# Attention and a cosine feed-forward in one kernel: scores of three units at a time, masks as products, tables ahead of loads

## The chip, the cores and the metric

The kernel runs on one core of a Trainium2 chip. The metric is the device time of one execution in microseconds. The engines that matter here: PE multiplies matrices into PSUM (eight banks), ACT (ScalarE) evaluates exponentials and sines and copies, DVE (VectorE) does elementwise work, POOL (GpSimd) makes small tables and issues the casting loads, and SP issues stores and transposing transfers.

## What is computed

Sliding-window attention with a linear distance bias for 8 batches, 8 heads, 576 positions and 64 features a head, and then a feed-forward layer with h * cos(h) as its activation:

```python
scores = scale * np.matmul(q, k.transpose(0, 1, 3, 2))          # scale = 1/8
rel = pos[:, None] - pos[None, :]
bias = slopes[:, None, None] * (-np.abs(rel))[None, :, :]       # slopes[h] = 2 ** -(h + 1)
mask = (rel >= 0) & (rel < 128)
scores = np.where(mask, scores + bias[None], -1e9)
attn = softmax(scores); x = attn @ v                            # x: 4608 tokens by 512
h = x @ w_in                                                    # 512 by 2048
out = (h * np.cos(h)) @ w_out                                   # 2048 by 512
```

## The kernel before

**Units.** Attention is cut into units of one batch, one pair of heads and one group of 256 query positions (G = 0 or 1), and a tail unit ("t") that holds the last 64 positions of all four pairs; nine units a batch. For each unit `scores` (L485 to L516) multiplies keys by queries. A head has 64 features, so the two heads of a pair lie in the two row halves of PE, each half writing a bank of its own: a unit of G = 0 is 2 x 256 + 2 x 128 columns in four matmuls, a unit of G = 1 has six matmuls, a tail sixteen. This mode of PE, with 64 active rows, is entered and left for every call of `scores`. `exps` (L521) takes the exponential on ACT into a buffer `p`, `mask` (L543) multiplies by `emask` on DVE, which holds exp(slope * distance) inside the window and 0 outside, `pv` (L567) multiplies by V with a column of ones that gives the sums, `norm` or `norm_two` divides on DVE (L632, L634 for one unit, L647, L649 for two at once), and `x_pe`, `x_pe_two` or `x_dma` transposes the result into `xT`.

**Chunks.** The 4608 tokens go through the feed-forward in nine chunks of 512. `moe1` (L738 PE, L744 ACT, L748 DVE), or `moe1_half` (L762, L767, L771) for chunk 0, makes g = h cos(h) bank by bank. `moe2` multiplies by `w_out`: plainly for chunk 0 (L823), else with seven products of sums of blocks (L879), whose sums `gsum` DVE makes (L813). Attention of later batches runs beside it: after the hidden layer of chunk c come QUOTA[c] units (9, 9, 11, 10, 10, 9, 5), an "exp phase", since ACT has to load another table between sines and exponentials. The first nine units run before chunk 0. Scores use banks 4 to 7 (`SB`), P times V banks 2 and 3 (`UB`), the output products banks 0 and 1 (`OB`); the hidden layer uses `UB` and `SB`.

**Order.** Nothing is ordered by hand. Each operation is recorded with the keys it reads and writes; `schedule` then reads a start time for each from the packed table `STARTS`, and with it, for operations that either ACT or DVE may do, the engine. On each engine the instructions stand in the order of these times, and waits are put where a dependence crosses engines.

**Head.** SP loads the first 256 positions of q in float32 (`load_first_q`, L317), which ACT and DVE cast (L321, L322). POOL issues, in this order: the first piece of k (L310), the identity (L374, L375), the second pieces of q and k (L310), the table of distances `dif` (`distances`, L381 to L388; float32, -1e6 outside the window), V and the four pieces of w_in (L329, L361), later loads. ACT makes the eight `emask` tables from `dif` (L431). PE runs nine warm-up products (L416), transposes q and k (L451), runs two more warm-ups, and starts on the scores; after the first two units come four `KEEP` products (L424), whose results nobody reads.

Of the kernel before, what the change touches and what calls it, by code (L numbers as in the profile page):

```python
# [30 lines left out]
    "c-o~_3v?7k7M%_O>$I}lyrVd&jB%(mF^)}$p`BmNBm)V<BtVRC3?U#pXoN{bfe~0_v#^HGLJXi7CH^2HBJ28J`M7FSR7Auzi"  # L31
    ">`PMD)?FS99B_8k|mkxecj0<nM?@iHl(NORn@C{_uY4^O@bCR#hzFzDnu_Z4LqqOM~tp!(zK43spEgAsq-12zXU-OPMJDJyG"
    "FE5pIUcU(+yf&S3rvpGe%5F#&6Q;gj4l!eBQRcM$dPi)^96f>ViXy3f+TUK??Ex_?UZoi}ePy7=cHHq$I;%TQatPH1&QW2^O"
    "tae}Jjg)c4bK!)TW`!4wg?M|;lc-=g*2U5i1e^=S8%0HKFT5F)~9wCJ7oq;rJU(~YU$Ap5fjNoV4^-LPssAdUm*EFfy}tAw*"
    "d7Qeoe16pEPbn`{)>S^6W#(6tWlXONuxu9u6i;kjBnHaLa0G)FilG}P);_)*m7dcDZ9r(4!VE#V{ro|J?*tM+_n`EuW83*8="
    "$!EHk4mzc89Ua&%w4zMuwl?8htQz#+Ux8CER0I<_)th;J>Pw`Lb42=R3H`3^f7EoIqwzE~c!-XZP4ReKaJtJ=QY6~LYnxudT"
    "2iY{OZ;n3P_N#|Cq;gFg(m<lm=Y-(O(<wBR?0%mA|%X7w3yCfF~!QV>om#H_IMI@6sj?)>zYk!F?DkAoO~M8`pY?ZK}&+x#p"
    "eL?Gq5G$8t8fpv5GY%jK*Icf~h~Pi>cRu_HIiL6+I)IF9yFxuY^QixA&I&<kLd$ghu1FUq~cRzZN0h4<e8h!7$s-eSb&KX-E"
    "t)p|FI+vN_$?oiFI0cikzBBz_SjUWbCQs`K<h*V?FHeB)@5gwsZPom=a?pW<gldkI%GAqK4vFwSNxxl}uTDU+G;{NSb*k0(P"
    "ue9_kjYX@!n!8R%o@C5?1%#Evp&F1C<({f&|`0Ww%oY7al^-RnAKA+Fy#@B)XK5wroS^Ag2O-gFoo%RzFNRV%~o4>i{LS<7%"  # L40
    "C7V_^mZgr8TIC_G!+9UbZx(uvjCNqxk#;JzFvt7Sq?-p%gk$PuG}qE#|FL!Rdk5wDUrKIDL_#)9-3V?{PAb5bpD#*i$x=e&U"
    "Z!Q(0+RVer9Mey#ijf`4-pl#nfX_SjewayrcxlF+iv%hDr`}6-lK}TfGHC7Ei1%nB}6PW^Vx(_oJMN-ql}^twxYy)t-gZ~f@"
    "VHIbQXxE)JAy<j){a3%5S;$#FoOA6_dYuYF2YJ=)T`MuHa+JZ?!!sy-gQ2R@j_^&Hv=@Mq-pHsah(p-uc(;@AQ~cu0BrvWr2"
    "wel@2(KV?yeE@<Mvtaj`t?OC89~_pBBd1@+dz%a0ZWWfh8nNq#r@3lLSXwg**^=1IT+W_cvY0&7kaG((t45RjIFAEb|G<$RC"
    "9;ABs@gsSDa^o5zO8MuP+9l8fTL@BY?@tdovPfpL<99mbFoHt%%Px-uuB`CJ?JE#gpd7CBh*Lip8#Ncz$DdQjd{fimDQ<Bx3"
    "i8la~m1}QjAla_lh&!?T$@NaJ{g`d^NICzC!?X6kOdnj7KLW-Me?tunuAb|FadMMdv?jaIfwnbrO1Z-Ua{B&2U_t;w|M>cwl"
    "Qr2(-C5bo-9!XEbz;ZMJe`GALM#&K2Fzs2Yg;jim{c(~%S<~P8BBDG7EcB>5pjuObE37>BBi=2GIS19=&8#BwiGH4*NKoT>R"
    "z1+k@p6bO*yTQ15WQ0P?_p|`hJk=_*by0sg6&%e~y0zANe_BVSX1vW94^-WQ1chm0<d3D*;&8yRrcB$kQZx(G2hJK`mf;&p*"
    "s$tM|TK%2?i7Spuu~x(Ds~RHFIU<o?|@lO0IgZ*x9NS4_G?XUHhue^M*eMMs`lt1~2(wx(^_&=|SxgwBu=sozmc)xNcM%j)|"
    "a)HZzR<?s$k8=ILwOuAvrvA~OgP}-j0(|51VdCr-A>{a5Uo-if&&j5u|(gi3oLL{lKOh14e1FuvP-K+I6nt|_9Std|UC4yxp"  # L50
    "i&!|iv49K{P8wbeNM$N-Yd*YiyAu}?5M_6k?x#%NTM9Z!c7P;jB8rG#{!Q6X8ybB_(e~^bu1RyC+IuBZWfFe^-&s@F<9p0|F"
    "G~<&-a-{Tncij6!;s0pP!QuO*B46)b6tg8m%Yzo)mr)F1N&aHO|Q=z0rS)UR=smq_8(l%!4<bv?|!x62#2X@uVfburqk&Vhb"
    "*TK9cCW=C!5`|ry;j;1i0GUKMe!}wdEDTKVCevrosJb)u<ci?UZRJ%McdxLAn@7iJW8Lgk_(8XBx;on8-x)TSTP9LyWjHkdm"
    "~D`f##aM3{_u>4*0D#Vj`>Pn}|c1gny7ncajd!ACp*+uf1^#Ixk6o)%qU_`OvBC8Cv2F?J$iolBb_PKO1aqdxwwU-CiCPET&"
    "$2oy3&A@-cH!!Re5D8$F75h61@h?U<?j0kLuUr9t8#oeuZIVzMcUW`9ZsG`#$C+{c85KP?dE?kKGz--NA$Ve)xR<04MhmEJ2"
    "+~B;-;+y?%$<t7o`e?(}bzd~jbior9TkJ&_*3kLskS;l>{a>{<=jQS~^pO$pNMp6lxt=~3oIes=6*U%Au2135^`33T&X0oY_"
    "l9XViju{A>~lOdR%WbzQxBQD+PU?_CKBI^q@&mku(6re)I$+0_>;0ZD`wed7sGaG-O~>o=;S#R>*lN|6<^nNiC-n@wEPTpua"
    "?ivT_w%pvtdESK`-|)**@L{Okw=D@&>T+M{vHKJ5))w@*Nb_())obsc!Fwj3UhMNEY-nMGbAekq-;%p0E3M=LgLXIlxu0JEv"
    "%Hc&bC*xG4!qm|0{IMuY519wlG0)#khvuZ4vp&4RNoZOw`)mpj*vug?xOI2)RNBI4HIjGzuX6|pwWbC7Tps7J>Mjbh5Kqd;W"
    "Z6*~pwAQ*M%Hdsi;n3q^+mac_v1P01IkTQOs&ORLoH~wURG~eq4X7g0*k}y>CC^;VA$q-&1R`1VD52;Y1P`B|!bEwwG1uA3k"  # L60
    "H_^;>S>AgV17&<=h^dS}4}Pim-Hr1UydD+;3)%A?fQyiEZ8rT<N%5<y;yv^X!^&S{fOYe?J9jj`^rloHE!*Z%i@e#(9JW^Z`"
    "U;pcMP2Sf;os#+8#6C>cT*dswwjZ=up2>xIom@G6!Zu&2s+%g!MJfdK>(uCMnl?kqlXj$@zVm7C8~&itfon5Ra4r=6p@nZ;`"
    "%b10zpztgDI}lqKW`6E+e^&R?HJsb3qBfM_GJ5qiWqhCo(8y{JSM|>lm*C8q^67%`f+iDdB|=*A%ny_lBzKQT0`}lkxPudVF"
    "o+(wbcFCG3+jJHJA$$NFglH95z7p+u2RZzx;k+*_Ml56*J3MW$zETS=&PiA^jGVk((_e(L{{(V(i!ZYkZA;`$!zjw<-+QZI!"
    "SEN}XW$Y6#{6j4t;^@I5p2ADr87Uwb<^GL5a{<(okkcb|f1frVqeyKhev9S{sFD2A8wMq#+wU5sYQk#9;vKr=Rk5}UD$M`s_"
    "vc&pWUbx7gG4-L^u$1xGPr*_s-gU?iwIA`rMZ4>)-WE{HqWm%%Jjh&YhVCz7eEHW((8?dE`^|3a^&`S&i4_)=LU!qdrsi)*v"
    "Em06a`h8fh*I&QsqS?WT7bk7QGH-f$&jn3txO`Iq8efyVc@b<;y<{BVjsh19d`?PuIdFtenn|PxFhF6`p?4~!4NokPfRh=KO"
    "4TC81rC%Ojy`4_CHg`1$z"
# [153 lines left out]
def bass_alibi_sliding__then__act_gcu_kernel(  # L222
# [8 lines left out]
    with ExitStack() as ctx:  # L231
# [32 lines left out]
        ob = [obuf[:, i, :] for i in range(NOB)]  # L264
        rec = [sb(f"rec{i}", [128, 8], F32) for i in range(2)]
        ident = sb("ident", [128, 128])
        halfpi = sb("halfpi", [128, 1], F32)
        dif = sb("dif", [128, 2, 128], F32)
# [3 lines left out]
        KEEP = 4  # L272
        QUOTA = [9, 9, 11, 10, 10, 9, 5]
# [39 lines left out]
        def load_first_q():  # L313

            t0, R, _ = PIECES[0][0]
            rows = bass.AP(q.tensor, q[0].offset, [[64 * R, 32], [64 * S, H], [1, 64 * R]])
            op("sp", [lambda e: e.dma_start(obuf[:, 0:2, :], rows)],  # L317
               w=[("ob", 0), ("ob", 1)], dma="hwq", occ=60, lat=500)
            for y, eng in enumerate(("dve", "act")):
                o = qB["q"][:, y, 0:512]  # L320
                op(eng, (lambda e, o=o, y=y: e.tensor_copy(o, ob[y])) if y == 0 else  # L321
                   (lambda e, o=o, y=y: e.activation(o, ob[y], ACTF.Copy)),  # L322
                   r=[("ob", y)], w=[("qB", "q", 0, y)], occ=(340, 450)[y], lat=(420, 560)[y],
                   pri=3)

        def load_v(b, order=range(NBLK)):
            for t in order:
# [5 lines left out]
                   occ=900, lat=740 * rows // 100)  # L333
# [94 lines left out]

        def masks():
# [56 lines left out]
        def scores(us, slot):  # L486

            def f(e):
                ins = None
                for n, (b, pr, G) in enumerate(us, slot):  # L490
                    banks = SB[2 * n:2 * n + 2]
                    if pr == "t":
                        for pr in range(NPAIR):
                            for half in range(2):
                                for x in range(2):
# [3 lines left out]
                                                   query_ap(b, x, pr, 4, 64), start=True, stop=True)  # L499
# [4 lines left out]
                    for (c0, c1, kc, qb, nb) in jobs:  # L504
                        for x in range(2):
                            ins = e.matmul(ps[:, banks[x], c0:c1], keys_ap(b, x, pr, kc),  # L506
                                           query_ap(b, x, pr, qb, 128 * nb), start=True, stop=True)
                return ins
            keys, held, occ = [], [], 0
            for n, (b, pr, G) in enumerate(us, slot):  # L510
                keys += tkeys((b, pr, G))
                held += [("B", x) for x in SB[2 * n:2 * n + 2]]
                occ += 250 if pr == "t" else 220 if G else 165
            if us[0] == (0, 0, 0):
                keys.append("warm2")
# [5 lines left out]
        def exps(u, n, table):  # L521
            b, pr, G = u
            banks = SB[2 * n:2 * n + 2]
# [414 lines left out]

        def attention(us, phase):

            for g in range(0, len(us), 2):
                two = us[g:g + 2]
                if phase < 0 or SINGLE:
                    for n, u in enumerate(two):
                        scores([u], n)
                        exps(u, n, 2 * phase + 2)
                        mask(u)
                else:
                    scores(two, 0)
                    for n, u in enumerate(two):  # L950
                        exps(u, n, 2 * phase + 2)
                    for u in two:
                        mask(u)
                if phase < 0 and g == 0:
                    keep()
                sets = [list(zip(two, OB if phase < 0 and g == 0 else UB))]
                if any(u[1] == "t" for u in two):
                    sets = [[s] for s in sets[0]]
                for set_ in sets:
                    pv(set_)  # L960
                    after = []
                    (b, pr, G), _ = set_[0]
                    if (PAIRN and phase >= 0 and len(set_) == 2 and set_[1][0] == (b, pr + 1, G) and set_[0][1] == UB[0]
                            and ucount[0] % 2 == 0):
                        n = ucount[0]
                        ucount[0] += 2
                        norm_two(set_, n)
                        if (S * b + 256 * G) // CH > phase + 1:
                            x_dma(set_[0][0], n)
                            x_dma(set_[1][0], n + 1)  # L970
                        else:
                            x_pe_two(set_, n)
                        continue
# [97 lines left out]
```

The softmax here doesn't subtract the row's maximum and nothing guards it: scores larger than these inputs give would overflow.

## Time and profile before

| | us |
|---|---|
| median of 5 runs | 302.45 (302.04 to 303.46) |
| the profiled execution | 302.49 |
| its span | 300.7 |
| PE busy, 2917 matmuls | 292.2 |
| DVE busy | 245.0 |
| ACT busy | 209.0 |
| POOL busy | 95.1 |
| mean of one L738 matmul of 512 columns | 0.379 |
| mean of one L744 cosine, one L748 product | 0.687, 0.686 |
| mean of an exponential of 128x768, of 128x1024 (L538) | 0.810, 1.025 |
| load of an ACT table | 1.283 |

The page gives for each engine its busy time, and the span in 40 slices of 7.5 us with the busy share in tenths. The timeline lists instructions in order of time, start first and then length, with the number of merged instructions after x and in brackets the idle time before them and what ended it. Matmuls overlap, so the length of a row of matmuls is longer than their spacing; the spacing is read from the starts of successive rows. The windows view gives for a stretch the busy time and count of PE, PE's weight load, DVE, ACT and POOL, then PE's granted clock, the mean share of the 16 DMA engines in use and the GB/s moved.

### The profile page before, as it was taken

What the parts mean: (1) busy time and instruction counts of PE and PEld (TensorE: products, weight loads), DVE (VectorE), ACT (ScalarE), POOL (GpSimd) and SP (SyncE); (2) the same over time, 40 slices, a digit from 0 to 9 for tenths busy, and PEclk for the clock granted to TensorE, in tenths of its full rate; (3) what the DMA queues carried; (4) which work ended last, traced back from release to release, by engine and by line L of the source; (5) the groups of instructions that cost most, each with busy time, mean ns of one, the idle gap of its engine ahead of it and who ended that gap; (6) DMA issues with size and microseconds to landing.
All of it is one profiled execution on the core that took longest, in us unless ns stands there. A gap on an engine that the chain in (4) does not pass through costs nothing.

```text
span 300.7 us, 7145 instructions
## 1 busy us (share of the span) xinstructions
PE 292.2 (97%) x2917; PEld 199.5 (66%) x2917; DVE 245.0 (81%) x513; ACT 209.0 (69%) x302; POOL 95.1 (32%) x122
## 2 busy tenths in 40 slices
PE   7779999999999999999999999999999999999996
PEld 2568745546774588547888886468656865566785
DVE  3878888879977998899988998899879966686781
ACT  5987777488766887787759766778667855755431
POOL 7930992059967501760195014000000000000000
PEclk9999999999999999999999999999999999999999
DMA  7999999999999999999899948972124213102033
GB/s 158 166 200 211 206 167 195 137 165 156 136 188 142 154 173 180 132 174 159 135 147 160 203 40 115 131 175 47 19 46 98 70 20 96 37 0 72 0 124 122
DMA packets 148065, 38.02 MB, mean 126 GB/s; under 512 B 133697, under 2 KB 146753, under 8 KB 148033
## 3 DMA queue, kind: packets, MB, share of 16 engines
q0 software_dynamic: 99344, 18.10, 77.4%
q1 hardware_dynamic: 48688, 19.47, 34.5%
q8 instruction: 23, 0.38, 0.5%
q14 instruction: 10, 0.07, 0.1%
HBM read 36.70 MB, written 9.44 MB: 153 GB/s over the span
## 4 chain that ended last, share of the span: by engine, by line
PE 91%; DMA 6%; POOL 1%; issue 0%; ACT 0%; ACTq 0%; POOLq 0%
PE ps L738 37%; PE ps L879 34%; PE ps L823 5%; PE ps L506 5%; DMA w_inb<-in_moe_w_in_dram 4%; PE ps L762 3%; PE ps L593 2%; DMA krows<-in_k_dram 2%; PE ps L596 2%; PE ps L451 1%; PE ps L497 1%; PE ps L580 1%; PE ps L582 1%; PE ps L700 1%; POOL w_inb L361 0%; PE ps L662 0%
## 5 line engine op out<-in xcount | busy, mean ns | idle before, releaser
L738 PE MATMUL ps<-xT,w_inb 128*128 128x512 bf16 (+1 forms) x576 | 129.0, 355 | 0.0
L744 ACT ACTIVATE cos<-ps,halfpi 128x512 f32<-128x512 f32 x128 | 82.7, 687 | 42.7 <-PE ps L738 30.8
L748 DVE TENSOR_TENSOR gT<-ps,cos 128x512 f16<-128x512 f32 x128 | 83.4, 686 | 19.4 <-ACT cos L744 18.1
L738 PEld LDWEIGHTS ps<-xT,w_inb 128*128 128x128 bf16 x576 | 55.2, 98 | 41.0 <-DVE gT L748 1.0
L538 ACT ACTIVATE p<-ps 128x768 bf16<-128x768 f32 (+1 forms) x64 | 56.0, 918 | 11.0 <-PE ps L506 8.1
L329 POOL DMA_DIRECT2D vp<-in_v_dram x40 | 34.0, 885 | 70.2 <-PE ps L596 29.1
L879 PE MATMUL ps<-wsum,gT 128*128 128x256 f16 x256 | 48.0, 273 | 0.0
L562 DVE TENSOR_TENSOR p<-p,emask 128x512 bf16<-128x512 bf16 (+2 forms) x96 | 41.9, 458 | 0.9 <-ACT p L538 0.4
L879 PE MATMUL ps<-w_outb,gT 128*128 128x256 f16 x256 | 42.4, 273 | 0.0
L879 PE MATMUL ps<-wsum,gsum 128*128 128x256 f16 x256 | 39.4, 273 | 0.0
L339 POOL DMA_DIRECT2D qnat<-in_q_dram x30 | 25.4, 893 | 17.6 <-DMA qt<-qnat 16.4
L879 PEld LDWEIGHTS ps<-w_outb,gT 128*128 128x128 f16 x256 | 24.5, 98 | 8.3 <-issue 0.5
L879 PEld LDWEIGHTS ps<-wsum,gT 128*128 128x128 f16 x256 | 23.9, 98 | 7.3 <-issue 0.6
L879 PEld LDWEIGHTS ps<-wsum,gsum 128*128 128x128 f16 x256 | 24.0, 98 | 4.9 <-issue 0.2
L339 POOL DMA_DIRECT2D knat<-in_k_dram x30 | 25.6, 928 | 2.0 <-DMA kt<-knat 1.4
L879 PE MATMUL ps<-w_outb,gsum 128*128 128x256 f16 x128 | 24.9, 273 | 0.0
L506 PE MATMUL ps<-qt,kt 64*128 64x128 bf16 (+1 forms) x320 | 18.8, 239 | 1.5 <-DVE kt L469 1.1
L593 PEld LDWEIGHTS ps<-vp,p 128*128 128x128 bf16 x256 | 16.2, 98 | 3.8 <-issue 1.0
L593 PE MATMUL ps<-vp,p 128*128 128x65 bf16 x256 | 18.3, 193 | 0.2 <-DVE p L562 0.2
L899 ACT ACTIVATE qrows<-ps 128x512 f32<-128x512 f32 (+1 forms) x18 | 9.9, 551 | 12.5 <-PE ps L879 12.5
L762 PE MATMUL ps<-xT,w_inb 128*128 128x256 bf16 x128 | 16.3, 273 | 1.8 <-DMA w_inb<-in_moe_w_in_dram 1.8
L506 PEld LDWEIGHTS ps<-qt,kt 64*128 64x128 bf16 x320 | 11.0, 94 | 9.6 <-issue 4.0
(81 smaller groups left out, 345.7 us busy)
## 6 DMA issues: line engine op xcount, KB each, us to landing
out_dram<-ob SPq DMA_DIRECT2D x32, 256.0 KB, 3.5
vp<-in_v_dram POOLq DMA_DIRECT2D x32, 128.0 KB, 10.2
qnat<-in_q_dram POOLq DMA_DIRECT2D x24, 128.0 KB, 8.3
knat<-in_k_dram POOLq DMA_DIRECT2D x24, 128.0 KB, 9.9
w_inb<-in_moe_w_in_dram POOLq DMA_DIRECT2D x4, 512.0 KB, 9.7
w_outb<-in_moe_w_out_dram POOLq DMA_DIRECT2D x4, 512.0 KB, 21.6
out_dram<-ob SPq DMA_DIRECT2D x8, 128.0 KB, 1.7
qrows<-in_q_dram POOLq DMA_DIRECT2D x1, 576.0 KB, 14.9
```

Of the source, the lines that this page charges most:

```text
L329: op("pool", [lambda e, t=t, rows=rows: e.dma_start(vp[b % 2][0:rows, t, :, 0:64], v[b, :, 128 * t:128 * t + rows, :].rearrange("h p d -> ...
L339: fns.append(lambda e, t=t, rows=rows: e.dma_start(nat[which][b % 2][0:rows, t, :, :], src[b, :, 128 * t:128 * t + rows, :].rearrange("h p ...
L506: ins = e.matmul(ps[:, banks[x], c0:c1], keys_ap(b, x, pr, kc), query_ap(b, x, pr, qb, 128 * nb), start=True, stop=True)
L538: op("act", lambda e: e.activation(P[i][:, :, 0:hi], src_[:, :, 0:hi], ACTF.Exp, scale=0.125), w=held + [("P", i)], occ=920 if G else 691, ...
L562: op("dve", lambda e, p=p, m=m: e.tensor_tensor(p, p, m, ALU.mult), r=[("P", i), ("EM", h0), ("EM", h1)], w=[("P", i)] if n != 1 else [("P ...
L593: ins = e.matmul(o, P[i][:, x, d0:d0 + 128], V[:, kc, h, 0:65], start=True, stop=not two)
L738: op("pe", lambda e, kc=kc, c0=c0: e.matmul(ps[:, bank, c0:c0 + n], w_in[:, kc, 128 * fc:128 * fc + 128], xT[:, kc, (r0 + c0) % XR:(r0 + c ...
L744: op("act", lambda e: e.activation(cosb[ci][:, :], ps[:, bank, :], ACTF.Sin, bias=halfpi[:, 0:1]), r=["halfpi"], w=[("B", bank), ("cos", c ...
L748: op("dve", lambda e: e.tensor_tensor(gT[gi][:, fc, :], ps[:, bank, :], cosb[ci][:, :], ALU.mult), r=[("cos", ci)], w=[("B", bank), ("g", ...
L762: op("pe", lambda e, i=i, fc=fc, kc=kc: e.matmul(ps[:, bank, 256 * i:256 * i + 256], w_in[:, kc, 128 * fc:128 * fc + 128], xT[:, kc, r0:r0 ...
L823: op("pe", lambda e, t=t, fc=fc, bank=bank: e.matmul(ps[:, bank, :], gT[gi][:, fc, 128 * t:128 * t + 128], w_out[:, fc, :], start=(fc == 0 ...
L879: op("pe", lambda e, t=t, fc=fc, bk=bk: e.matmul(ps[:, bk, 256 * t:256 * t + 256], lhs(fc, t), rhs(fc), start=first and fc == 0 and (last ...
```

## The change

1. Scores in threes. `scores` takes a list of units with a pair of banks for each, in `SLOTS` (the two halves of `SB`, and `UB`). A new `attention` takes three units in its first call where the number of units of the phase is odd, with `UB` as the third pair, and two after that. QUOTA becomes 9, 9, 11, 11, 9, 9, 5. `attend` holds what followed the masks before; finished units wait in a list, so that P times V and the normalization take two units of neighbouring pairs together wherever they can.
2. Masks as products. The first nine units have a function of their own, `first_attention`. For its four units with G = 0 the mask on DVE is gone: `biases` puts 8 * slope * distance into the banks on PE, as a product of a scaled identity (`scaled_identities`, eight small operations on DVE, in the space of an output buffer) and `dif`, now bfloat16, and the scores are added on top.
3. Tables ahead of the second loads. `distances` and `identity` stand before the second loads of q and k.
4. The second warm-up is gone and KEEP is 0. The planner's latency of two loads is changed, and `STARTS` is new throughout, so that instructions move on every engine.

```diff
-        KEEP = 4
-        QUOTA = [9, 9, 11, 10, 10, 9, 5]
+        KEEP = 0
+        QUOTA = [9, 9, 11, 11, 9, 9, 5]
...
+        scaled = obuf[:, 2, :].bitcast(BF16).rearrange("p (h c) -> p h c", h=H)
...
-        dif = sb("dif", [128, 2, 128], F32)
+        dif = sb("dif", [128, 2, 128])
...
+        def scaled_identities():
+            for h in range(H):
+                op("dve", lambda e, h=h: e.tensor_scalar(
+                    scaled[:, h, :], ident[:, :], 8.0 * slopes[h], None, ALU.mult),
+                   r=["ident"], w=[("scaled", h)], occ=95, lat=180, pri=3)
+
+        def biases(u, banks):
...
+                for c0, n in ((0, 2), (256, 2 if G else 1)):
+                    for x in range(2):
+                        ins = e.matmul(ps[:, banks[x], c0:c0 + 128 * n], scaled[:, 2 * pr + x, :],
+                                       dif[:, 0:n, :], start=c0 == 0, stop=False,
+                                       skip_group_check=True)
...
+        SLOTS = [SB[0:2], SB[2:4], UB]
...
+        def first_attention(us):
             for g in range(0, len(us), 2):
                 two = us[g:g + 2]
+                for n, u in enumerate(two):
+                    if u[2] == 0:
+                        biases(u, SLOTS[n])
+                    scores([u], [SLOTS[n]], u[2] == 0)
+                    exps(u, SLOTS[n], 0)
+                    if u[2] != 0:
                         mask(u)
...
+        def attention(us, phase):
+
+            waiting, at = [], 0
+            while at < len(us):
+                size = 3 if at == 0 and len(us) % 2 else 2
+                group = us[at:at + size]
+                at += size
+                slots = ([UB] if size == 3 else []) + SLOTS[0:2]
+                scores(group, slots)
+                for u, banks in zip(group, slots):
+                    exps(u, banks, 2 * phase + 2)
+                for u in group:
+                    mask(u)
+                waiting += group
+                while waiting:
...
+                    attend(list(zip(waiting[:1 + pair], UB)), phase)
+                    waiting = waiting[1 + pair:]
...
         load_qk("k", k, 0, 0)
+        distances()
         identity()
+        scaled_identities()
         load_qk("q", q, 0, 1)
         load_qk("k", k, 0, 1)
-        distances()
         constants()
...
-            if n == 0:
-                warm(2, 384, "warm2")
...
-        attention(every[0:9], -1)
+        first_attention(every[0:9])
```

## The prediction, made before the changed kernel ran

> **What bounds the kernel now.** I read the page's busy shares and slices first, then the chain of waits, the timeline around one visit to the scores, and last the first 26 us by engine and DMA.
>
> ```profile
> PE 292.2 (97%) x2917; PEld 199.5 (66%) x2917; DVE 245.0 (81%) x513; ACT 209.0 (69%) x302; POOL 95.1 (32%) x122
> ...
> PE   7779999999999999999999999999999999999996
> ...
> PE 91%; DMA 6%; POOL 1%; issue 0%; ACT 0%; ACTq 0%; POOLq 0%
> ```
>
> PE is full from the fourth slice (22.6 us) to the last, and the chain is PE for 91% and DMA for 6%. A busy PE is not PE at its peak, so the spacing of its starts has to be read. In the timeline (start, length, matmuls):
>
> ```profile
> 70.60 2.13 PE L879 MATMUL ps<-w_outb,gT 128*128 128x256 f16 x18
> 72.66 0.50 PE L506 MATMUL ps<-qt,kt 64*128 64x256 bf16 x8
> 73.10 0.50 PE L879 MATMUL ps<-w_outb,gT 128*128 128x256 f16 x3
> ...
> 78.81 0.61 PE L506 MATMUL ps<-qt,kt 64*128 64x256 bf16 x12
> 79.36 0.39 PE L879 MATMUL ps<-wsum,gsum 128*128 128x256 f16 x2
> 79.59 0.39 PE L662 MATMUL ps<-ident,xnat 128*128 128x128 bf16 x4
> ```
>
> A product of 256 columns takes 0.109 us from start to start. Eighteen would take 1.97; the scores start after 2.06. So entering the 64-row mode costs 0.09. Eight score matmuls hold PE for 0.44 us and twelve for 0.55: four more (two pairs of 128 columns) add 0.11, hence the 768 columns of the eight stream in 0.33, and leaving the mode costs about 0.10. **One visit to the scores costs 0.19 us beyond its columns.** Nothing else is loose: between 30 and 290 us each stretch of 10 us shows PE busy for 9.96 or more.
>
> The PE stream starts for good when the last piece of w_in lands:
>
> ```profile
> 19.75 1.16 PE L762 MATMUL ps<-xT,w_inb 128*128 128x256 bf16 x9 [1.52 <-DMA w_inb<-in_moe_w_in_dram]
> 25.45 3.45 PE L762 MATMUL ps<-xT,w_inb 128*128 128x256 bf16 x30 [0.23 <-DMA w_inb<-in_moe_w_in_dram]
> 5.00:6.00 1.00, 0.44 (x17) 0.43 (x16) 0.59 (x2) 1.00 (x3) 0.33 (x2) 1.00 1.23 203
> 24.00:25.00 1.00, 1.00 (x13) 0.90 (x11) 0.90 (x2) 0.59 (x2) 0.00 (x0) 1.00 1.14 209
> ```
>
> The last columns of the two window rows are the DMA share and GB/s: the engines are already full at 5 us and still full at 25. So w_in is late because of the bytes ahead of it in POOL's queue, not because it is issued late (12.4 to 13.2 us). **End = landing of the fourth w_in piece (25.45) + PE work left after it (to 297.5, the start of the last product) + 3.2 us of last reads and stores.**
>
> **The change part by part.** *Scores in threes.* In the instruction order, after the wait for the fourth piece, score matmuls are the same 392, but in 28 visits where there were 34: 6 x 0.19 = **-1.14 us**.
>
> *Order at the head.* Before that wait the old order has 54 half-chunk products (L762), the new one 62. PE has the time for them: between 19.75 and 25.22 the old order does 40 such products, a set of P times V and four pairs of transposes; the new one does 46 products and two pairs (46 x 0.109 + 4 x 0.055 = 5.2 us), because it puts its last early P times V ahead of the second piece's wait, where PE sat idle for 1.5 us. Eight fewer remain: 8 x 0.109 = **-0.87 us**. The 0.23 us idle before the piece is not won, since the piece still decides.
>
> *Transposes.* 56 on PE after that point become 52 (two moved to the head, two become one DMA transpose): 4 x 0.055 = **-0.22 us**.
>
> *Bias products, KEEP, second warm-up.* Four units get 4 products each (512 + 256 columns, 0.33 us a unit, 1.3 us), and two more visits of 0.19; removed are 4 KEEP products of 0.216 and two warm-ups (0.5 us busy). That is some +0.3 us on PE before 19 us, under the idle time in front of the second piece; without that cover, 0.3. Removing the fillers could let PE's clock drop, but the longest gap in this trace, from about 18.2 to 19.75, is followed by nine matmuls in 1.16 us, full speed; I expect none longer: 0.
>
> *VectorE and ScalarE.* The eight masks go (4 x 0.410 + 4 x 0.282 = 2.8 us) and eight tensor_scalar 128x128 come. No row shows one; a MEMSET of 128x128 words took 0.165 us, a quarter of the 128x512 CAST 0.11: about 1 us in all. Fourteen more pairs of units are normalized as one (0.205 + 0.689 instead of twice 0.171 + 0.419): -4.0 us. ScalarE changes by under 1 us. None of this is on the path; it widens the margin.
>
> *Tables ahead of the second loads.* POOL now makes the distances (4.18 to 5.46 us in the old row, 1.28 us) and the identity (0.54 us) straight after the first k load, at 2.16. So the second q load is issued at 2.16 + 1.28 + 0.54 = 4.0 us where it was 2.70, and the second k load at 4.75. The V loads follow at about 5.45 (they were 6.00, held by a MEMSET that now comes earlier), and w_in behind them; but the queue is full, so only a hole in it counts. These rows give the old issue-to-landing times:
>
> ```profile
> qrows<-in_q_dram POOLq DMA_DIRECT2D x1, 320.0 KB, 5.2
> krows<-in_k_dram POOLq DMA_DIRECT2D x1, 320.0 KB, 6.2
> krows<-in_k_dram POOLq DMA_DIRECT2D x1, 256.0 KB, 4.8
> ```
>
> They landed at 6.1, 7.9 and 9.7 us, 1.8 apart for 320 KB: back to back. At about 200 KB per us the first k load moved its data from some 4.2 to 5.6, 2.9 us after its issue at 1.32. If the second q load takes as long to its first byte, that is 6.9: a hole of 1.3 us, and w_in 1.3 us later. *The rule against the row:* the Trainium skill, DMA: Bandwidth & Descriptors (Specifications), puts the first byte of a GpSimd DMA at about 1 us. By it data would flow at 5.0, before the first load is through: no hole, total -2.2; by the row of the first k load +1.3, total -0.9. A third measurement lies between: a V load issued at 176.31 with an empty queue,
>
> ```profile
> 177.00:177.50 0.50, 0.50 (x23) 0.48 (x22) 0.50 (x2) 0.21 (x1) 0.19 (x1) 1.00 0.00 0
> 177.50:178.00 0.50, 0.50 (x14) 0.41 (x7) 0.50 (x2) 0.32 (x1) 0.00 (x0) 1.00 0.20 37
> ```
>
> moved its first bytes 1.2 to 1.7 us after issue, which makes a hole near 0.1. The q load resembles the first k load in shape, but that was the queue's first transfer and shared the engines with a 512 KB load. I take **+0.6 us**, ends 0 and 1.3.
>
> **Sum:** -1.14 - 0.87 - 0.22 + 0.6 = -1.6 us. The profiled execution took 302.49 (span 300.7 and 1.8 around it), 0.04 above the median: 302.49 - 1.6 = **300.9 us**.
>
> **Where the stall could be instead.** Three units of scores need six PSUM banks, two need four. *The second rule against a row:* the Trainium skill, TensorEngine Tiling (Array Packing), Gotcha 1: PSUM Pressure, warns that row tiles writing to different banks raise the pressure on PSUM. In the old order PE's visit at 72.66 came 0.31 us after the last bank was read:
>
> ```profile
> 69.87 2.48 DVE L748 TENSOR_TENSOR gT<-ps,cos 128x512 f16<-128x512 f32 x4
> ```
>
> (it ends at 72.35). From the second phase on the new order puts 17 or more products between the last hidden-layer matmul and the scores (18 here in the old): 1.85 us, against 0.16 + 0.687 + 0.686 = 1.53 for the matmul's way out (its mean of 0.379 less its spacing of 0.216), the cosine and its product. By the row nothing waits: 0. By the rule all six banks must be free, and one gsum (0.687) standing ahead of the last product on VectorE would eat the margin of 0.3 and leave 0.4 us at every phase.
>
> **Rivals.** (1) *The banks decide (slower).* A late cosine product holds the three-unit scores at the head of each of the seven phases; behind that instruction all of PE waits. At 0.5 us: 7 x 0.5 = 3.5, 300.9 + 3.5 = 304.4. It overtakes the gain at 1.6 / 7 = 0.23 us a phase. For it: at one phase (104.34) the old scores began while a bank outside their four was still to be read until 105.3. Against: VectorE has less to do. (2) *The head's ScalarE chain decides.* ScalarE is busy for 9.83 of the 10 us to 20. The second k load comes later by the hole, and the transposes of the second q now stand between the scores of units 0 and 1, so exponentials, table load and first cosine (19.2 us) slide. Past about 20.5 the banks of the half-chunk run out before w_in does; at 1.2 us more: 302.1. For it: the full ScalarE row. Against: one copy and two waits on masks left the chain. (3) *Fewer visits save nothing*, the drain being paid elsewhere in a longer visit: -0.5 in all, 302.0. Against: x12 against x8 above adds its columns alone.
>
> **How the numbers follow.** Forecast 0.60 (its own range 300.2 to 301.6 by the ends of the hole), banks 0.18, ScalarE chain 0.17, visits 0.05. This measurement tells 0.3%, 0.9 us, from no change: faster is below 301.5, slower above 303.4. The forecast gives 0.57 faster and 0.03 same; rival 2 splits 0.05, 0.10, 0.02; rival 1 gives 0.02 same and 0.16 slower; rival 3 is 0.05 same. Together 0.62, 0.20, 0.18. The range 300.0 to 303.4 takes in the unknown ends and rivals 2 and 3, and leaves out the banks and little else.
>
> **What would show it.** The fourth w_in wait ending at 25.5 to 26.7 with 66 half-chunk products behind it; 28 visits to the scores after that, each still 0.19 above its columns; PE gaps after 26 us of 0.3 us in sum, as now. Wrong if the scores' first matmul in a phase waits for VectorE (rival 1), or if PE waits for VectorE or ScalarE between 20 and 26 us (rival 2).

## The result, and the profile after

| | before | after |
|---|---|---|
| median, us | 302.77 (75 runs) | 301.7 (40 runs, 301.03 to 303.53) |
| ratio | | 0.996, 95% interval 0.9949 to 0.9971 |
| profiled execution, us | 302.49 | 301.07 |
| its span, us | 300.7 | 299.3 |

The change makes the kernel faster by 1.1 us at the median (0.9 to 1.5 by the interval); 300.9, a gain of 1.6, was forecast. The profiled execution of after, 301.07, is one of the fastest of its 40. That matters below: what this trace shows is after at its best.

Busy shares, slices and the chain of waits of the changed kernel:

```profile
PE 291.8 (97%) x2925; PEld 200.5 (67%) x2925; DVE 240.4 (80%) x478; ACT 209.5 (70%) x300; POOL 95.1 (32%) x122
...
PE   6899999999999999999999999999999999999996
...
PE 94%; DMA 2%; DVE 1%; POOL 1%; issue 1%; ACT 0%; POOLq 0%; DVEq 0%; ACTq 0%
```

DMA's share of the chain fell from 6% to 2%. The 4% that were w_in's are gone, and VectorE, which had none, has 1%. PE is full one slice earlier than before.

The timeline of PE in the head (start, length, matmuls, in brackets the idle time before and what ended it):

```profile
10.43 0.75 PE L481 MATMUL ps<-ident,krows 128*64 128x128 bf16 x20 [0.17 <-DMA krows<-in_k_dram]
...
12.20 0.25 PE L623 MATMUL ps<-vp,p 128*128 128x65 bf16 x3 [0.32 <-issue]
...
14.39 0.40 PE L730 MATMUL ps<-ident,xnat 128*128 128x128 bf16 x4 [0.64 <-DVE xnat L664]
...
16.39 1.05 PE L792 MATMUL ps<-xT,w_inb 128*128 128x256 bf16 x8 [0.25 <-DVE xT L740]
...
19.83 0.20 PE L623 MATMUL ps<-vp,p 128*128 128x65 bf16 x1 [0.39 <-DVE xT L740]
...
20.33 1.15 PE L792 MATMUL ps<-xT,w_inb 128*128 128x256 bf16 x9
...
24.27 3.44 PE L792 MATMUL ps<-xT,w_inb 128*128 128x256 bf16 x30
```

The old waits for w_in (1.52 us at 19.75, 0.23 us at 25.45) have no successor: the last row runs through the landing of the fourth piece (25.07) without a gap, and the first product that needs this piece, the 63rd half-chunk product, starts 0.63 us after it, at 25.70. PE is now late for another reason, a chain in its own head: a load, P times V, the norm on VectorE, xT, half-chunk products. The "issue" at 12.20 hides a load: by the trace's landing times the second V load lands at 12.11.

Scores in threes, the first visit after the hidden layer:

```profile
70.73 0.93 PE L909 MATMUL ps<-w_outb,gT 128*128 128x256 f16 x7
71.59 0.67 PE L538 MATMUL ps<-qt,kt 64*128 64x256 bf16 x12
72.19 0.72 PE L909 MATMUL ps<-w_outb,gT 128*128 128x256 f16 x5
```

Twelve score matmuls hold PE for 0.60 us and nothing waits for a bank. From the 55th half-chunk product (the 63rd in after) to the start of the last product the trace has 272.05 us before and 270.49 after.

The second loads, now behind the tables, from issue to landing:

```profile
qrows<-in_q_dram POOLq DMA_DIRECT2D x1, 320.0 KB, 4.5
krows<-in_k_dram POOLq DMA_DIRECT2D x1, 320.0 KB, 5.7
krows<-in_k_dram POOLq DMA_DIRECT2D x1, 256.0 KB, 4.7
```

Issued 1.26 us later, they land 0.53 (q) and 0.72 us (k) later in these two traces. Landings scatter as much, though: in the three traces with the old order the k load, issued at 3.46 or 3.47 each time, lands at 9.66, 10.19 and 11.15, and in the seven traces whose loads are ordered as in after at 10.17 to 11.00. The hole in the queue is there. Windows of after, then of before; the last two numbers are the DMA share and GB/s:

```profile
5.50:6.00 0.50, 0.46 (x16) 0.46 (x16) 0.18 (x3) 0.50 (x2) 0.50 (x2) 1.00 1.56 80
6.00:6.50 0.50, 0.50 (x22) 0.43 (x18) 0.28 (x1) 0.50 (x3) 0.50 (x2) 1.00 0.36 61
```

```profile
5.50:6.00 0.50, 0.42 (x16) 0.43 (x16) 0.20 (x1) 0.50 (x3) 0.00 (x1) 1.00 1.21 198
6.00:6.50 0.50, 0.50 (x22) 0.43 (x18) 0.24 (x1) 0.50 (x3) 0.50 (x1) 1.00 1.19 210
```

About 130 KB are missing in that microsecond, some 0.65 us at 200 KB per us, and all seven traces with the new order of loads have the hole (30 to 122 GB/s in these two windows). Yet the fourth w_in piece lands at 25.07, before 25.41 (24.95 to 25.71 in the seven traces, 25.05 to 26.24 in the three with the old order). What made up the time is open. The old kernel moves less at 10 to 11 us (134 and 100 GB/s, after 151 and 157), and after issues V and w_in 0.48 us earlier. But the earlier issue is not shown to be what fills that dip: the run 'before_v_early' (below) issues the first V load at 5.59 and w_in at 7.34, where after has 5.52 and 7.27, and its dip only comes half a microsecond later:

```profile
10.50:11.00 0.50, 0.50 (x20) 0.41 (x16) 0.50 (x3) 0.50 (x2) 0.50 (x2) 1.00 0.85 89
11.00:11.50 0.50, 0.41 (x8) 0.29 (x9) 0.50 (x4) 0.50 (x2) 0.50 (x2) 1.00 0.68 96
```

### The profile page after: what moved, and what is told of

Read it like the earlier page. It is cut to its first block, busy times and chain, and to the rows that moved or that the text cites. A ratio compares the mean times of both kernels' runs of the same rounds, so it can differ in the third digit from the quotient of the medians.

```text
span 299.3 us, 7125 instructions
## 1 busy us (share of the span) xinstructions
PE 291.8 (97%) x2925; PEld 200.5 (67%) x2925; DVE 240.4 (80%) x478; ACT 209.5 (70%) x300; POOL 95.1 (32%) x122
## 4 chain that ended last, share of the span: by engine, by line
PE 94%; DMA 2%; DVE 1%; POOL 1%; issue 1%; ACT 0%; POOLq 0%; DVEq 0%; ACTq 0%
PE ps L768 37%; PE ps L909 34%; PE ps L792 5%; PE ps L853 5%; PE ps L538 5%; PE ps L623 3%; PE ps L626 2%; DMA krows<-in_k_dram 2%; PE ps L481 1%; PE ps L692 1%; PE ps L528 1%; PE ps L610 1%; PE ps L612 1%; DVE xnat L664 1%; POOL krows L310 0%
## 5 line engine op out<-in xcount | busy, mean ns | idle before, releaser
L909 PE MATMUL ps<-wsum,gT 128*128 128x256 f16 x256 | 50.8, 273 | 0.1
L592 DVE TENSOR_TENSOR p<-p,emask 128x512 bf16<-128x512 bf16 (+2 forms) x88 | 39.0, 471 | 3.1 <-ACT p L568 2.6
L909 PE MATMUL ps<-w_outb,gT 128*128 128x256 f16 x256 | 39.7, 273 | 0.0
L909 PE MATMUL ps<-wsum,gsum 128*128 128x256 f16 x256 | 37.2, 273 | 0.0
L909 PEld LDWEIGHTS ps<-wsum,gsum 128*128 128x128 f16 x256 | 24.8, 98 | 4.6 <-ACT qrows L929 0.2
L909 PE MATMUL ps<-w_outb,gsum 128*128 128x256 f16 x128 | 26.1, 273 | 0.0
L679 DVE TENSOR_TENSOR xnat<-ps,rec 128x512 bf16<-128x512 f32 x28 | 19.3, 691 | 1.3
L623 PE MATMUL ps<-vp,p 128*128 128x65 bf16 x256 | 18.0, 193 | 0.8 <-DVE xT L740 0.4
L623 PEld LDWEIGHTS ps<-vp,p 128*128 128x128 bf16 x256 | 15.6, 97 | 4.0 <-issue 1.1
L626 PE MATMUL ps<-vp,p 128*128 128x65 bf16 x192 | 16.9, 193 | 0.0
```

The lines of the kernel that those rows point to most:

```text
L592: op("dve", lambda e, p=p, m=m: e.tensor_tensor(p, p, m, ALU.mult), r=[("P", i), ("EM", h0), ("EM", h1)], w=[("P", i)] if n != 1 else [("P ...
L623: ins = e.matmul(o, P[i][:, x, d0:d0 + 128], V[:, kc, h, 0:65], start=True, stop=not two)
L626: ins = e.matmul(o, P[i][:, x, p0:p0 + 128], V[:, kc - 1, h, 0:65], start=False, stop=True)
L679: op("dve", lambda e: e.tensor_tensor(o, U[:, :, :, 0:64], rv[:, :, :, None].broadcast_to([128, 2, 4, 64]), ALU.mult), r=[("rec", n // 2 % ...
L909: op("pe", lambda e, t=t, fc=fc, bk=bk: e.matmul(ps[:, bk, 256 * t:256 * t + 256], lhs(fc, t), rhs(fc), start=first and fc == 0 and (last ...
```

## The experiments

The theories: **V**, the landing of the second V load starts PE's stream; **K**, the second k load and the work behind it do; and the prediction's view, w_in's last piece does. Beside them stand the terms of the sum: visits, fillers, masks, PE's later waits. All times of the trace below are of one execution each, all ratios are to the kernel before.

### What a visit to the scores costs

```diff
-                for banks, (b, pr, G) in zip(slots, us):
+                for n, (banks, (b, pr, G)) in enumerate(zip(slots, us)):
+                    if n:
+                        e.matmul(ps[:, banks[0], 0:64], ident[slice(0, 128), :], ident[slice(0, 128), 0:64],
+                                 start=True, stop=True, skip_group_check=True)
```

The second run has the same lines with slice(0, 64).

> The changed kernel, with one idle product of 64 columns on all 128 rows put between the units of every visit to the scores (35 places), so that PE leaves the 64-row mode and comes back 35 times more. If a visit costs 0.19 us beyond its columns: 35 x (0.19 + 0.03 for the columns) = +7.7 us over the changed kernel, about 309.4 us, ratio to the kernel before 1.022. If the number of visits is worth nothing (rival 3): only the columns, 35 x 0.03 = +1.0 us, 302.7 us, ratio 1.000.

> As the run with 128-row products, with the same 35 idle products on 64 rows, so that the mode stays and only columns and instructions are added. Both theories: 35 x 0.03 = +1.0 us over the changed kernel, 302.7 us, ratio 1.000. If instead any product between units of scores costs 0.2 us whatever its mode, it is as slow as the other run, ratio 1.02.

Measured: 309.53 us (ratio 1.0227, 1.0193 to 1.0261) with 128 rows, 302.2 us (0.9985, 0.9966 to 1.0004) with 64. The timeline of the run with 128 rows, then the first and the next row of the same visit with 64:

```profile
72.85 0.34 PE L541 MATMUL ps<-qt,kt 64*128 64x256 bf16 x4
73.12 0.20 PE L524 MATMUL ps<-ident 128*128 128x64 bf16 x1
73.26 0.34 PE L541 MATMUL ps<-qt,kt 64*128 64x256 bf16 x4
73.53 0.20 PE L524 MATMUL ps<-ident 128*128 128x64 bf16 x1
73.67 0.34 PE L541 MATMUL ps<-qt,kt 64*128 64x256 bf16 x4
73.94 0.72 PE L912 MATMUL ps<-w_outb,gT 128*128 128x256 f16 x5
```

```profile
71.79 0.34 PE L541 MATMUL ps<-qt,kt 64*128 64x256 bf16 x4
...
72.44 0.72 PE L912 MATMUL ps<-w_outb,gT 128*128 128x256 f16 x5
```

The visit now takes 1.09 us; with 64-row products it takes 0.65. The difference, 0.44 for two places, is 0.22 each. Over the run it is (309.53 - 302.2) / 35 = 0.21; a wait of 0.68 us for a load at batch 6, which the first trace has and the second has not, would change this by 0.02. The columns alone cost 0.5 us in time where 1.0 was expected. A visit's price is real, it is the change of mode, and rival 3 is out.

### Which load starts the stream

The second loads ahead of the tables again (both, or q alone), and the casts of the first q ahead of the scaled identities and half of the tables:

```diff
+        for o in [o for o in self.all if o.dma in ("ldq1", "ldk1")][:2]:
+            o.start = dif[0].start - 1
...
```

> The changed kernel with the second q and k loads issued ahead of the tables again (and the casts of the first q ahead of the scaled identities and tables on DVE and ACT, so that nothing waits for a late table). Theory A (the start of PE's unbroken stream is set by the chain from the second k load, landed at 10.38 us, through transposes, scores, P times V and the norm): the k load lands near 9.7 and the stream starts 0.3 to 0.7 earlier, 301.0 to 301.4 us, ratio 0.994 to 0.996. Theory B (ScalarE's or VectorE's own work in the head sets it): no gain, 301.7 or up to 0.8 more since the tables come 1.5 later, ratio 0.996 to 0.999. Prediction's view (the hole in the queue makes w_in late and w_in decides): w_in lands 0.7 earlier and the time falls by 0.6, ratio 0.994.

> The changed kernel with only the second q load issued ahead of the tables, which then come 0.76 us later; the second k load stays behind them. Theory A: the k load follows the q load in the queue without a hole and lands near 9.7 to 10.0, the stream starts 0.2 to 0.6 earlier, ratio 0.994 to 0.996. Theory B: 0 to +0.4, ratio 0.996 to 0.998.

Measured: 302.2 us (0.9986, 0.9965 to 1.0007) and 301.91 us (0.9972, 0.9957 to 0.9986). No gain from either, against theory A. The reason is not that the landing doesn't count but that an earlier issue did not bring an earlier landing: issued at 2.89 instead of 4.72, the k load landed at 10.63 instead of 10.38, inside the scatter shown above. The stream followed the landings all the same, which asked for a direct test of V, by putting a w_in piece ahead of it:

```diff
+        piece = [o for o in self.all if o.w == (("wi", 0),)][0]
+        for o in [o for o in self.all if o.w in ((("v", 0, 0),), (("v", 0, 1),))][0:2]:
+            o.start = piece.start + 1
```

> The changed kernel with the first piece of w_in (512 KB) issued ahead of the first two V loads. Theory V (in every trace so far the first P times V starts 0.09 us after the second V load lands, so this landing starts PE's stream): V lands about 2.6 later, near 14.7, the stream starts about 2.5 later and so does the end: 304.2 us, ratio to the kernel before 1.005. Theory K (the second k load and the work behind it decide, V being there just in time by chance): less than 1 us of it is seen, ratio below 1.000. Prediction's view (w_in's last piece decides): nothing, since the bytes ahead of that piece are the same: 301.7 us, ratio 0.996.

Measured: 305.37 us (1.0071, 1.0047 to 1.0095), 3.7 us over after, where V expected 2.5. The timeline:

```profile
15.34 0.33 PE L626 MATMUL ps<-vp,p 128*128 128x65 bf16 x3 [3.11 <-issue]
```

V landed at 15.25, the first P times V started 0.09 later and everything behind it slid. In the profiled executions the 63rd product comes 4.58 us later than in after: 3.14 are V's landing, 1.45 the stretch behind it, in which PE's clock is granted at 0.50 from 14.82 to 21.65 us, after most of the 3.1 us of idling. All ten executions have a mean granted clock of 0.988 to 0.994, where 39 of the 40 of after have 0.999 or 1.000. By the traces:

| run | second V load landed | first P times V | 63rd half-chunk product | last product |
|---|---|---|---|---|
| after | 12.11 | 12.20 | 25.70 | 296.19 |
| loads_first | 12.35 | 12.44 | 25.93 | 296.74 |
| tail (below) | 12.72 | 12.81 | 26.30 | 296.85 |
| q_first | 12.93 | 13.02 | 26.51 | 298.67 |
| v_late | 15.25 | 15.34 | 30.28 | 300.80 |

In the first four the 63rd product comes 13.49 or 13.50 us after the first P times V, and where no later wait comes between, the last product comes 270.5 to 270.8 us after that. These four rows alone would fit theory K as well, since the second k load lands 1.72 to 1.74 us ahead of the V load in each; 'v_late', in which V was moved by itself, decides for V. So in these traces **the end of the changed kernel is the landing of the second V load, plus 0.09, 13.5 and 270.5, plus the last reads and stores.** That landing spreads from one execution to the next, 11.9 to 12.7 us in the seven traces whose loads are ordered as in after. The rule ends where V lands early: in the next run PE is free for P times V at 11.73, so that 0.4 to 0.5 us is the most that an earlier V could win from after, and no run shows such a gain.

Half of V first, heads 0 to 3 of both blocks ahead of heads 4 to 7:

```diff
-        load_v(0, range(2))
+        load_first_v()
```

> The changed kernel with each of the first two V loads cut into heads 0 to 3 and heads 4 to 7, and the first halves of both issued first, so that P times V of the first two units waits for half the bytes. Theory V: the first P times V starts at about 11.9 instead of 12.20, when PE is through with the scores, and the whole stream 0.3 earlier: 301.4 us, ratio 0.9955. Theory K: it starts where it did, or what follows does: 301.7 us, ratio 0.9965. The trace tells these apart, the times hardly.

Measured: 302.46 us (0.9987, 0.9959 to 1.0015). The first P times V did start earlier, at 11.73. But four issues of 0.73 us on POOL instead of two of 0.88 put w_in's first piece 1.2 us later in the queue; it landed at 16.79 instead of 14.63, and PE waited for it:

```profile
16.83 0.39 PE L815 MATMUL ps<-xT,w_inb 128*128 128x256 bf16 x1 [1.80 <-DMA w_inb<-in_moe_w_in_dram]
```

```profile
14.00:16.00 2.00, 1.03 (x16) 0.58 (x16) 1.68 (x6) 1.77 (x3) 2.00 (x4) 1.00 2.23 161
16.00:18.00 2.00, 1.17 (x8) 0.89 (x9) 0.53 (x2) 0.32 (x2) 2.00 (x3) 0.72 1.45 197
18.00:20.00 2.00, 2.00 (x17) 1.47 (x16) 1.71 (x4) 0.98 (x2) 2.00 (x4) 0.50 1.26 205
```

The third number from the end, PE's clock, falls to 0.50. Its twelve times lie in two groups, eight from 301.15 to 302.65 and four from 303.91 to 304.45; the profiled one is of the second. The mean granted clock of the executions nearly sorts them: all eight of the first group have 1.000, three of the second 0.994, which is what the 3.41 us at 0.50 in the trace make of its 302.7 us. The fourth of the second group, 303.96, has 1.000; its cause is open. The eight have a median of 302.09, no better than after; in the trace the wait for w_in takes what the earlier P times V gives.

### Does w_in decide in the old kernel

```diff
+        cast = [o for o in self.all if o.w == (("qB", "q", 0, 0),)][0]
+        for o in [o for o in self.all if o.w == (("vinit", 0),)]:
+            o.start = min(o.start, cast.start - 1)
```

> The kernel before with one change: the MEMSETs of the V buffer stand ahead of the cast on VectorE, so that the V loads and w_in are issued about 0.5 us earlier. If the hole in the queue at 10 to 11 us is what late issues cost: the fourth w_in piece lands 0.2 to 0.4 before 25.41 and the end comes as much earlier, 302.4 us, ratio 0.9985 to 0.9993. Prediction's view (the queue is full, issue times do not matter): landing and time as before, ratio 1.000.

Measured: 302.64 us, ratio 0.9987 (0.9965 to 1.0008). In its trace the fourth piece landed at 25.05 instead of 25.41, and the last product started 0.14 earlier. The landing is as expected, but it lies inside the scatter of landings, and the dip in the queue stayed (above); the time cannot tell 0.36 us from none. What the trace does show is that the fourth piece need not decide even in the old order. PE waits for the second piece here, and the 55th product, the first that needs the fourth, starts without a wait, 0.26 us after the landing:

```profile
20.00 1.16 PE L765 MATMUL ps<-xT,w_inb 128*128 128x256 bf16 x9 [1.31 <-DMA w_inb<-in_moe_w_in_dram]
...
25.31 2.89 PE L765 MATMUL ps<-xT,w_inb 128*128 128x256 bf16 x25
```

So the two pieces decide within a few tenths of a microsecond of each other.

### Masks and fillers

The bias products left out, the four masks back on VectorE right behind their exponentials; then the same with the bias products kept and overwritten by the scores (the cut shown is of the first; the second keeps the line with `biases`):

```diff
-                    if u[2] == 0:
-                        biases(u, SLOTS[n])
-                    scores([u], [SLOTS[n]], u[2] == 0)
+                    scores([u], [SLOTS[n]])
                     exps(u, SLOTS[n], 0)
-                    if u[2] != 0:
-                        mask(u)
+                    mask(u)
```

> The changed kernel with the bias products left out and the masks of the first four units (G = 0) back on VectorE. Theory V and K: first P times V still at V's landing, but VectorE has 1.6 us more between 9 and 14 us and its norms come later: PE's waits for xnat and xT grow by 0.2 to 0.8, ratio 0.997 to 0.999. Prediction's view (both costs lie under the wait for w_in): 0, ratio 0.9965.

> As the run with the masks of the first four units back on VectorE, but the 16 bias products stay on PE and the scores then overwrite what they wrote, so that only VectorE's part is undone and PE stays as busy. Theory C (the run without the products lost its time to PE's granted clock, 0.50 at 9 to 12 and 16 to 21 us, after PE had been idle): the clock stays at 1.00 and only 0.2 to 0.8 us over the changed kernel are left, ratio 0.997 to 0.999. Theory D (the masks on VectorE and the later copies and norms cost the time by themselves): again about 2 us over it, ratio 1.003.

Measured: 304.05 us (1.0032, 1.0007 to 1.0057) and 303.69 us (1.0024, 1.0000 to 1.0049). Both took more than was expected. In the profiled executions the clock did what theory C said, at 16 to 20 us in the run without products and in the run with them:

```profile
16.00:18.00 2.00, 1.52 (x17) 1.00 (x18) 1.97 (x7) 1.61 (x3) 2.00 (x4) 0.50 1.37 206
18.00:20.00 2.00, 2.00 (x14) 1.43 (x13) 1.59 (x5) 1.85 (x3) 2.00 (x3) 0.50 1.24 205
```

```profile
16.00:18.00 2.00, 1.69 (x24) 1.08 (x22) 2.00 (x6) 1.98 (x5) 2.00 (x4) 1.00 1.32 204
18.00:20.00 2.00, 2.00 (x44) 1.73 (x42) 2.00 (x7) 0.95 (x2) 2.00 (x3) 1.00 1.25 207
```

But the profiled execution with the products is the fastest of its twelve (302.69), and one of only three with the clock at 0.999 or 1.000 throughout; the other nine have 0.989 or 0.994, so the products did not keep the clock in most executions. The three have a median of 302.85, 1.15 us over after. The trace agrees: its 63rd product comes 14.48 us after the first P times V, where after has 13.49, so 0.99 us are VectorE's. The other 0.8 of the 2.0 us goes with the fall of the clock in the nine. So theory D is right on rather more than half of the loss, and theory C on the rest; the 0.2 to 0.8 us that C left to VectorE are too few. In the filled run:

```profile
13.75 0.62 PE L549 MATMUL ps<-qt,kt 64*128 64x256 bf16 x12 [0.64 <-DVE kt L510]
15.77 0.40 PE L741 MATMUL ps<-ident,xnat 128*128 128x128 bf16 x4 [0.93 <-DVE xnat L675]
```

The copies of k and the norms stand behind the masks on VectorE, and PE waits for them. (The masks were put where the new order leaves room, not where the old order had them.) The difference of the two runs, 0.36 us at the median, is within their intervals.

The old kernel without its fillers:

```diff
-                    keep()
...
-                warm(2, 384, "warm2")
```

> The kernel before without its two second warm-up products and its four KEEP products, whose results nobody reads, and with nothing in their place. Theory C: PE's clock falls to one half from about 8.5 us, as in the run without bias products; 2 to 4 us of PE's head are lost, of which the 1.5 us of waiting for the second w_in piece cover most: 0 to +2 us, ratio 1.000 to 1.007, and the granted clock shows the stretch. Prediction's view (the fillers can go at no cost): 0, clock 1.00 throughout.

Measured: 302.92 us, ratio 1.0001 (0.9984 to 1.0019): nothing, as predicted. The profiled execution, 303.99 us, is the slowest of twelve, and has a clock of 0.50 from 10 to 20 us. Seven of the twelve have a mean granted clock of 0.983 to 0.994, against three of the 29 executions of the kernel before beside them; the seven have a median of 302.89, the other five of 302.96. So the fillers do hold the clock, as theory C says, and what is lost without them lies under the wait for w_in nearly always.

### PE's later waits

```diff
+        later = [self.all[k] for k in (2223, 2224, 932)]
+        later[0].start = later[1].start = self.all[2219].start
+        later[2].start = self.all[861].start + 1
```

> The changed kernel with three instructions moved: at 246 us the two products that wait for VectorE's output read stand behind four products that do not, and at 107.5 us one block sum of VectorE stands behind the masks that P times V waits for. If PE's short waits after 26 us are what the gain fell short by: the 0.29 and 0.18 us of idle at these two places go and the end comes 0.4 to 0.5 earlier, 301.2 us, ratio 0.995. Rival: each wait only moves on to the next place where VectorE is late: 0 to 0.1, ratio 0.9965.

> The changed kernel with the three moves of the run 'tail' and, beside them, two MEMSETs of VectorE (a V buffer's and a K buffer's zeros, 0.38 and 0.09 us in its chain at 13.06 and 16.91) moved to its idle time at 8 us. In every trace with the changed kernel's order the 63rd half-chunk product starts 13.49 us after the first P times V. If VectorE's chain from P times V over the norms to xT is what fills these 13.49 us: they shrink by 0.1 to 0.4 and the end comes as much earlier than in 'tail', 301.2 to 301.5 us, ratio 0.994 to 0.9955. Rival: ScalarE's exponentials or w_in's second piece hold the later steps: 13.49 us stay, ratio 0.9964.

Measured: 301.64 us (0.9964, 0.995 to 0.9978) for the three moves, 301.99 us (0.9942, 0.9921 to 0.9964; the kernel before beside it had 303.27) with the MEMSETs moved too. Both waits of 'tail' are gone from its trace, but the time of after is kept. In 'memset' the 0.64 us wait for xnat became 0.27, and a new one took up what it gave:

```profile
14.54 0.40 PE L735 MATMUL ps<-ident,xnat 128*128 128x128 bf16 x4 [0.27 <-DVE xnat L669]
15.61 0.39 PE L543 MATMUL ps<-qt,kt 64*128 64x256 bf16 x6 [0.35 <-ACT p L573]
```

The 13.49 us became 13.44: the rival, with ScalarE as the next limit. Neither version is shown to beat after.

Both traces have something larger, at 178.59 and here at 179.82:

```profile
179.82 0.51 PE L543 MATMUL ps<-qt,kt 64*128 64x256 bf16 x8 [1.65 <-issue]
```

The trace's landing times name it. It is the first visit of batch 6, and the transposing load of its q landed 0.09 us before. Landing of the last of its q and k loads and first use, by the traces:

| | q and k of batch 6 landed | first scores of batch 6 | slack |
|---|---|---|---|
| before | 173.61 | 179.86 | 6.25 |
| after | 177.50 | 177.63 | 0.13 |
| tail | 178.50 | 178.59 | 0.09, PE idle 0.27 |
| v_half | 180.94 | 181.03 | 0.09, PE idle 0.71 |
| memset | 179.74 | 179.82 | 0.09, PE idle 1.65 |

Eight of the ten experiments on the changed kernel have this slack of 0.09 us, that is, their scores start as soon as the load is there; in 'q_first' the scores of batch 4 wait as well (1.31 us at 119.25). The old order has 6.1 to 6.3 us of slack in its three traces. So the new order brought in a wait that the profiled execution of after just misses. The last of these loads is not issued later than it was (170.58 in after, 171.26 before), but takes 6.92 us to land where it took 2.35; why is open. Issuing it earlier was not tried.

## Why the prediction was right, and where it was not

**Visits, -1.14.** Right. The traces have the 28 visits forecast, and the price measured by itself is 0.21 to 0.22 us, so six are worth 1.3.

**Order at the head, -0.87.** Right on the eight products: at 25.70 the new order starts its 63rd half-chunk product, where the old one starts its 55th at 25.45. Wrong on "PE has the time for them" and "the piece still decides", and this is the first half of the step that failed. The last early P times V was to run in PE's idle time ahead of the second piece (19.75). It waits for VectorE's xT until 19.83, so the 46 products behind it start only at 20.33. With the two pairs of transposes they take 5.37 us, close to the 5.2 reckoned, and when the fourth piece lands at 25.07 five of the 62 have not started. That piece is only 0.63 us ahead of its use, so w_in is close behind the new limit.

**Transposes, -0.22.** The trace has 54 of them on PE from the 55th product on, not 56, and 52 in after: -0.11.

**Tables ahead, "I take +0.6 us".** This is the other half. The mechanism given, a hole in the queue and w_in later by it, half happened: the hole is there (80 and 61 GB/s), where the Trainium skill's figure of about 1 us to the first byte (DMA: Bandwidth & Descriptors, Specifications) left none: the q load was issued at 3.96, the first of its packets of 1280 bytes starts at 5.45 in the trace, 1.5 us after issue, and the queue stays thin until 6.5, 2.5 us after issue. The row of the first k load (2.9) fits the second of these, the V load of the third measurement (1.2 to 1.7) the first. But w_in came 0.34 us earlier. "The queue is full, so only a hole in it counts" overlooked that the old queue had a dip of its own at 10 to 11 us. The term measured +0.25 (25.70 against 25.45) in the profiled executions, and it belongs to the V load and VectorE's chain behind it.

**"None of this is on the path; it widens the margin"** (VectorE and ScalarE). Wrong for the new order: once w_in no longer decides, VectorE's work in the head does, and putting four masks back, where the new order leaves room for them, costs 2.0 us, more than the whole change brought; rather more than half of it is VectorE's chain, the rest goes with the fall of PE's clock.

**Fillers, 0.** The time is right. For the old order the reason is not: without fillers the clock does fall in most executions, and only the wait for w_in hides it. In the new order, which has none, the clock holds in 39 of 40.

**"PE gaps after 26 us of 0.3 us in sum, as now".** Too low. The three gains as measured (1.29, 0.87 and 0.11) should have cut the 272.05 us by 2.27; the trace has 1.56 less. The 0.7 are short waits of PE in the new order: beyond the spacing that their columns need, its starts lose 1.0 us after 26 us, against 0.31 before, the two largest of them (0.29 and 0.18) at the places that 'tail' mended. Its trace has 0.2 us less there, its time no gain that can be told.

**The sum.** In the profiled executions the last product starts 1.32 us earlier: -1.29 - 0.87 - 0.11 + 0.25 + 0.7. So the sum is near because two errors partly cancel, 0.35 too much for the hole and 0.7 too little for the waits; that is luck, not reckoning. The median misses the 300.9 by 0.8, of which 0.3 is the kernel before itself, 302.77 by 75 runs where the forecast had 302.45; the gain is 1.1 where it had 1.6. Two costs that vary from one execution to the next point that way, V's landing and batch 6's load, which the profiled execution just escapes. That they make up the 0.6 us between it and the median was not measured.

**Rivals.** No phase head waits for a bank (1): PE's only idle times between 26 and 290 us, 0.11 us at 108.99 and 0.13 at 246.65, are not ahead of scores. Visits do save (3). Rival 2 named the right place, a chain in PE's own head in place of w_in, and the wrong engine: it is the V load and VectorE. Its sign, a wait between 20 and 26 us, did not show; the last wait of the head ends at 19.83.

## What to carry to other kernels

When a change pulls work ahead of the wait that decides, work out when the work itself will be ready, load by load: the next thing that is late is often a transfer or an engine that had 1 to 6 us of slack under the old wait. Compare landing and first use of every load in the two orders, not only of those that the diff moves, and over several traces, since one load landed here up to 1.5 us apart at the same issue time. And price a mode change by doubling it: idle products with and without the change give the cost to a few hundredths of a microsecond.

## What the hardware showed that was not expected

- Loads issued 1.8 us earlier landed no earlier (k: 10.63 against 10.38; one trace each, and landings scatter by up to 1.5 us at one and the same issue time). The engines were fed without a hole, at 155 to 202 GB/s between 5.5 and 8 us where the old kernel had 195 to 210. Why is open.
- PE's clock fell to one half at the end of a wait of 1.80 us in 'v_half', and kept 1.00 through one of 1.52 us in the kernel before. The low stretches in the head last 3.41 us, or two or three times that, to 0.01 us ('v_half' one, 'v_late' two, 'masks_dve' one and then two, 'before_nofill' three), and in the 3.41 us ahead of each PE is busy for 0.82 to 1.78 us. In 'v_half':

```profile
13.47:16.88 3.41, 1.26 (x21) 0.70 (x18) 2.18 (x7) 2.30 (x4) 3.41 (x6) 1.00 1.95 171
16.88:20.29 3.41, 3.41 (x28) 2.60 (x29) 2.23 (x5) 1.30 (x2) 3.41 (x5) 0.50 1.28 205
```

  The Trainium skill (TensorE: Matmul & The Clock Gate, Part 1) speaks of an idle window of about 3.4 us that runs freely; the length agrees, but none of these stretches was wholly idle. How much work in one would have kept the clock was not measured.
